# Sliding-window attention into a SwiGLU block: natural token order, 32-bit transposes, 128-row stores and a rebuilt start

## The chip, the cores and the metric

The kernel runs on one core of a Trainium2 chip. The metric is the device time of one execution in microseconds (us). Each run lists the execution that was profiled and several more; medians below are over all of them.

Names used below: TensorE (PE in the profile, with PEld for its weight loads), VectorE (DVE), ScalarE (ACT), GpSimd (POOL), SyncE (SP; its queue, which issues all the DMAs here, is SPq).

## The reference

```python
# q, k, v: (8, 8, 576, 64) fp32; window 64; weights (512, 1536) and (1536, 512)
scores = q @ k.transpose(0, 1, 3, 2) / sqrt(64)
rel = pos[:, None] - pos[None, :]
scores = where((rel >= 0) & (rel < 64), scores, -1e9)
attn = softmax(scores)
x = (attn @ v).transpose(0, 2, 1, 3).reshape(4608, 512)
g, val = x @ w_gate, x @ w_val
out = (g * sigmoid(g) * val) @ w_out
```

## The kernel before

The work is cut into 36 groups of 128 tokens (`NG`), 18 blocks of 256 tokens for loads of q, k, v (`NB`), and 9 tiles of 512 tokens for the feed-forward part. Everything is scheduled by hand: each engine runs its instructions in program order. After a start of about 147 us comes the main loop `for w in range(8, 36)`. One step of it does three gate/value column blocks, the projection of one earlier group, and the attention of a group four to six steps ahead.

To load two neighbouring tokens as one run of 512 bytes, partition r of a loaded block holds tokens 2r and 2r+1. This order (even tokens, odd tokens) goes through the whole kernel, up to the stores, which have to undo it:

```python
def load(n, src, nm, eng):
    ...
    eng.dma_start(
        x_f[o // 2:(o + m) // 2].rearrange("r h c d -> r h (c d)"),
        src[b, :, s:s + m, :].rearrange("h (r c) d -> r h (c d)", c=2),
    )

def turned(n, nm):                       # k and q of a block: 8 bf16 transposes each
    x_b = cast_qk.pop((nm, n))
    tp = ps_a.tile([P, 2, 4, P], BF16, name="tp", tag="a")
    for c in range(2):
        for p in range(4):
            nc.tensor.transpose(tp[:, c, p, :], x_b[:, c, P * p:P * p + P], identb[:])
    return tp

def products(g, via_pe=False):           # attention output of a group, then x turned
    ...
    if not via_pe:                       # groups 8 to 35
        sp.dma_start_transpose(out=xT[t][:, :, off:off + P], in_=x_b[:])
        return
    tp = ps_a.tile([P, 4, P], BF16, name="xtp", tag="a")   # groups 0 to 7
    for p in range(4):
        nc.tensor.transpose(tp[:, p, :], x_b[:, P * p:P * p + P], identb[:])
    act.copy(xT[t][:, :, off:off + P], tp[:])

def project(t, s, ps, tag):
    ...                                  # 12 matmuls of 512 columns, eviction by ScalarE
    n0 = 512 * t + P * s
    for i in range(2):
        sp.dma_start(
            out[n0 + 64 * i:n0 + 64 * i + 64, :].rearrange("(x c) f -> c x f", c=2),
            os_[64 * i:64 * i + 64, :],
        )
```

The softmax here doesn't subtract the row's maximum and nothing guards it: scores larger than these inputs give would overflow.

## Time and profile before

Median 452.41 us (three runs, 449.06 to 455.61). The profiled execution has a span of 452.1 us.

The main reading is by stretches: the start, the main loop with the last four projections, and the end after the last matmul. I date the boundary between start and loop by the first projection matmul inside the main loop, because it is easy to find.

| stretch | before |
|---|---|
| up to the first projection of the main loop | 153.4 us |
| from there to the last matmul | 279.8 us |
| after the last matmul | 19.0 us |

The first view is the table by stretches of the kernel before. Each line has the stretch, its length, then for each engine the busy time and number of instructions, then the granted TensorE clock (1.00 is full), the mean busy share of the 16 DMA engines, and GB/s.

```profile
core 0: us, PE busy (x) PEld busy (x) DVE busy (x) ACT busy (x) POOL busy (x), PEclk, DMA share, GB/s
0.00:147.00 147.00, 101.64 (x787) 70.00 (x788) 89.25 (x215) 48.38 (x97) 78.19 (x157) 0.86 0.67 163
147.00:433.00 286.00, 271.15 (x1736) 140.96 (x1733) 154.05 (x308) 103.04 (x172) 141.46 (x246) 0.97 0.46 93
395.00:433.00 38.00, 38.00 (x177) 17.11 (x175) 15.10 (x22) 10.15 (x17) 0.00 (x0) 1.00 0.11 36
433.00:452.00 19.00, 0.15 (x1) 0.00 (x0) 0.00 (x0) 0.60 (x1) 0.00 (x0) 0.57 0.12 48
```

Look at the last two lines. From 395 us on there is nothing left to load, and from 433 us on nothing left to compute. The stores alone are running, at a DMA share of 0.11 to 0.12. Two sixteenths are 0.125, so two of the sixteen engines work and fourteen idle. The Trainium skill says why ("DMA: Bandwidth & Descriptors", "Why a DMA increments its semaphore by 16 and not by 1"): a DMA is spread over the largest k up to 16 that divides the size of the slowest dimension on both sides. The store above has the slowest dimension `c`, of size 2. This trace agrees with that rule.

The next view is the instruction timeline of TensorE in the main loop of the kernel before. Columns: start, span of the piece (of a pipelined group, so use the differences of the starts), engine, line, what is computed, and the number of instructions.

```profile
205.48 0.61 PE L119 MATMUL tp<-identb,q_fb 128*128 128x128 bf16 x8
205.93 2.75 PE L273 MATMUL o_ps<-wo,hT 128*128 128x512 bf16 x12
208.51 1.03 PE L248 MATMUL g_ps<-xT,wg 128*128 128x512 bf16 x4
```

The eight bf16 transposes of a q block take 0.45 us from start to start (56 ns each), twelve matmuls of 512 columns 2.58 us. So TensorE is at its pace wherever nothing makes it wait. Where it does wait, the chain of waits shows a DMA transpose of x (columns: start, length, what):

```profile
223.69 0.70 DVE sg L259
...
224.61 7.57 DMA xT<-x_b
...
232.31 1.02 PE g_ps L248 x4
```

The queue of SyncE around the same time (start, length, what is issued) shows that the transpose is issued behind loads, and takes 4.46 us merely to be issued:

```profile
219.90 1.57 SPq L83 DMA_DIRECT2D q_f<-in_q_dram  x1
221.56 2.96 SPq L83 DMA_DIRECT2D v_f<-in_v_dram  x2
224.61 4.46 SPq L230 DMA_TRANSPOSE xT<-x_b  x1
229.16 1.09 SPq L281 DMA_DIRECT2D out_dram<-os__2762  x2
```

### The profile page before, as it was taken

The numbers are of one execution on the slowest core, as the hardware profiler recorded it, in microseconds if no ns is written. First come the engines' busy times: TensorE is split into PE (matmuls) and PEld (weight loads), VectorE is DVE, ScalarE is ACT, GpSimd is POOL, SyncE is SP. The second block draws the span as 40 slices with busy tenths as digits, with TensorE's granted clock in tenths as the row PEclk, the third lists the DMA queues.
The fourth block names the chain that finished last, engine by engine and source line by source line (L and its number), as shares of the span: only waits on it lengthen the run. The fifth ranks groups of instructions, "written<-read, shape, count | busy, mean of one in ns | idle before, by whom it ended". The sixth has DMA issues, their size and how long they took to land.

```text
span 452.1 us, 6976 instructions
## 1 busy us (share of the span) xinstructions
PE 372.9 (82%) x2520; PEld 211.0 (47%) x2520; DVE 243.3 (54%) x522; ACT 152.0 (34%) x270; POOL 219.7 (49%) x403
## 2 busy tenths in 40 slices
PE   2568689779853999699979988997999999999930
PEld 2355446556542555255535544553455554444410
DVE  5767868783431657266646554464457555646200
ACT  3243324424330343334424342433343433333210
POOL 6892330601997749464847554664648460000000
PEclk9988789889965999999999996999899999999975
DMA  8994809700599556615755763386363442211111
GB/s 254 323 261 161 259 0 259 162 1 20 158 71 184 142 129 129 134 47 133 138 116 117 103 131 87 109 102 130 81 130 85 52 51 38 45 36 33 38 48 45
DMA packets 82290, 51.30 MB, mean 113 GB/s; under 512 B 16720, under 2 KB 76112, under 8 KB 82256
## 3 DMA queue, kind: packets, MB, share of 16 engines
q1 hardware_dynamic: 82256, 50.87, 50.9%
q8 instruction: 19, 0.31, 0.3%
q14 instruction: 15, 0.12, 0.1%
HBM read 37.75 MB, written 9.44 MB: 104 GB/s over the span
## 4 chain that ended last, share of the span: by engine, by line
PE 54%; DMA 15%; DVE 10%; POOL 9%; ACT 3%; issue 3%; SPq 2%; POOLq 0%; DVEq 0%; ACTq 0%
PE g_ps L248 17%; PE v_ps L248 15%; PE o_ps L273 13%; DMA v_f<-in_v_dram 6%; DMA xT<-x_b 4%; PE ao_ps L219 4%; DMA k_f<-in_k_dram 3%; PE tp L119 2%; DMA out_dram<-os__4942 2%; DVE x_b L224 2%; POOL vbd_101 L108 2%; POOL E_102 L193 1%; SPq L83 1%; DVE sg L259 1%; POOL vbd_100 L108 1%
## 5 line engine op out<-in xcount | busy, mean ns | idle before, releaser
L259 DVE SCALAR_TENSOR_TENSOR sg<-th,g_ps 128x512 f32<-128x512 f32 (+1 forms) x123 | 76.5, 622 | 131.1 <-ACT th L253 130.5
L248 PE MATMUL g_ps<-xT,wg 128*128 128x512 bf16 (+1 forms) x492 | 120.9, 371 | 21.6 <-issue 7.5
L248 PE MATMUL v_ps<-xT,wv 128*128 128x512 bf16 (+1 forms) x492 | 118.7, 366 | 0.0
L253 ACT ACTIVATE th<-g_ps 128x512 f32<-128x512 f32 (+1 forms) x123 | 67.0, 545 | 142.0 <-PE g_ps L248 131.4
L273 PE MATMUL o_ps<-wo,hT 128*128 128x512 bf16 x432 | 98.6, 379 | 0.0
L264 DVE TENSOR_TENSOR hT<-sg,v_ps 128x512 bf16<-128x512 f32 (+1 forms) x123 | 76.3, 621 | 10.3
L248 PEld LDWEIGHTS <-wg 128*128 128x128 bf16 x492 | 48.8, 102 | 65.6 <-issue 18.5
L248 PEld LDWEIGHTS <-wv 128*128 128x128 bf16 x492 | 50.1, 102 | 50.1 <-issue 4.8
L273 PEld LDWEIGHTS <-hT 128*128 128x128 bf16 x432 | 41.2, 98 | 44.6
L224 DVE TENSOR_TENSOR x_b<-ao_ps,r 128x256 bf16<-128x256 f32 x72 | 30.6, 425 | 2.5
L108 POOL CAST vbd_98<-v_f 32x256 bf16<-32x256 f32 x48 | 20.5, 427 | 14.7 <-DMA v_f<-in_v_dram 12.9
L108 POOL CAST vbd_96<-v_f 32x256 bf16<-32x256 f32 x48 | 18.8, 393 | 17.8 <-DMA v_f<-in_v_dram 16.0
L193 POOL TENSOR_TENSOR E_102<-E_102,mask 128x512 bf16<-128x512 bf16 (+2 forms) x16 | 16.1, 1027 | 23.2 <-ACT E_102 L192 23.1
L108 POOL CAST vbd_100<-v_f 32x256 bf16<-32x256 f32 x48 | 18.9, 395 | 15.0 <-DMA v_f<-in_v_dram 13.2
L99 POOL CAST k_fb<-k_f 128x1024 bf16<-128x1024 f32 x16 | 16.6, 1037 | 19.1 <-DMA k_f<-in_k_dram 18.4
L223 DVE RECIPROCAL r<-ao_ps 128x4 f32<-128x4 f32 x72 | 12.7, 176 | 23.2 <-PE ao_ps L219 23.1
L193 POOL TENSOR_TENSOR E_104<-E_104,mask 128x512 bf16<-128x512 bf16 x14 | 15.8, 1149 | 16.5 <-ACT E_104 L192 16.4
L119 PE MATMUL tp<-identb,k_fb 128*128 128x128 bf16 x144 | 12.7, 240 | 12.8 <-DVE k_fb L99 7.8
L193 POOL TENSOR_TENSOR E_105<-E_105,mask 128x512 bf16<-128x512 bf16 x14 | 15.8, 1153 | 13.9 <-ACT E_105 L192 13.9
L193 POOL TENSOR_TENSOR E_103<-E_103,mask 128x512 bf16<-128x512 bf16 x14 | 15.8, 1153 | 12.5 <-ACT E_103 L192 12.5
L108 POOL CAST vbd_97<-v_f 32x256 bf16<-32x256 f32 x48 | 20.3, 423 | 2.2
L108 POOL CAST vbd_101<-v_f 32x256 bf16<-32x256 f32 x48 | 19.1, 399 | 2.2
(148 smaller groups left out, 450.1 us busy)
## 6 DMA issues: line engine op xcount, KB each, us to landing
k_f<-in_k_dram SPq DMA_DIRECT2D x12, 512.0 KB
q_f<-in_q_dram SPq DMA_DIRECT2D x12, 512.0 KB
v_f<-in_v_dram SPq DMA_DIRECT2D x12, 512.0 KB
w_f<-in_moe_w_gate_dram SPq DMA_DIRECT2D x4, 768.0 KB
w_f<-in_moe_w_val_dram SPq DMA_DIRECT2D x4, 768.0 KB
wo_f<-in_moe_w_out_dram SPq DMA_DIRECT2D x4, 768.0 KB
k_f<-in_k_dram SPq DMA_DIRECT2D x4, 384.0 KB
q_f<-in_q_dram SPq DMA_DIRECT2D x4, 384.0 KB
```

What stands on the lines that cost most here:

```text
L99: eng.tensor_copy(x, y)
L108: eng.tensor_copy(vb[64 * a + 32 * c:64 * a + 32 * c + 32, i % 2, :, 64 * a:64 * a + 64], v_f[32 * i:32 * i + 32, a::2, c, :],)
L119: nc.tensor.transpose(tp[:, c, p, :], x_b[:, c, P * p:P * p + P], identb[:])
L193: eng.tensor_mul(e, e, mask[:, lo:hi, :].unsqueeze(1).to_broadcast([P, 2, hi - lo, 64]))
L219: nc.tensor.matmul(o_ps[:, i, :], w, x, start=(n == 0), stop=(n == len(parts) - 1))
L223: dve.reciprocal(r[:], o_ps[:, :, P:VW])
L224: dve.tensor_mul(x_b[:, 256 * h:256 * h + 256].rearrange("r (p a d) -> r p a d", p=2, a=2), o_ps[:, :, 0:P].rearrange("r p (a d) -> r p a ...
L248: nc.tensor.matmul(ps[:, 0:n], w[:, c, P * m:P * m + P], xT[t][:, c, c0:c0 + n], start=(c == 0), stop=(c == 3),)
L253: act.activation(th[:, 0:n], g_ps[:, 0:n], AF.Tanh, scale=0.5)
L259: dve.scalar_tensor_tensor(sg[:, 0:n], th[:, 0:n], 1.0, g_ps[:, 0:n], ALU.add, ALU.mult)
L264: dve.tensor_mul(hT[t][:, m, c0:c0 + n], sg[:, 0:n], v_ps[:, 0:n])
L273: nc.tensor.matmul(o_ps[:], hT[t][:, c, P * s:P * s + P], wo[:, c, :], start=(c == 0), stop=(c == 11),)
```

## The change

The intent: keep tokens in natural order, so that a result tile is stored as 128 whole rows; pack two bf16 tokens into one 32-bit word, so that a block of q or k needs four fp32 transposes instead of eight bf16 ones; take the masks off GpSimd; turn all of x on TensorE; do the attention of four groups before the first gate/value work; and keep the TensorE clock up with dummy matmuls while the first loads run. Cut to its core:

```diff
-    KR, VR, ER, QR = 3, 6, 4, 3
+    KR, VR, ER, QR = 3, 3, 3, 3
-    wst = ctx.enter_context(tc.tile_pool(name="wst", bufs=4))
+    wst = ctx.enter_context(tc.tile_pool(name="wst", bufs=6))     # weights in 256-column pieces
+    def load_v(n):                                                # 256-byte runs
+        x_f = stage.tile([P, 2, H, D], FP32, name="v_f", tag="v_f")
+        for i in range(2):
+            for r, m, b, s, t in segments(256 * n + P * i, P, 1):
+                sp.dma_start(x_f[r:r + m, i], v[b, :, s:s + t, :].rearrange("h r d -> r h d"))
+    def pack(n, nm, eng):                                         # two tokens in one 32-bit word
+        x_w = cast.tile([P, H * D], FP32, name=nm + "w", tag=nm + "w")
+        y = x_w[:].bitcast(BF16).rearrange("r (h d c) -> r h c d", h=H, c=2)
+        ...copy x_f to y
     def turned(n, nm):
-        for c in range(2):
-            for p in range(4):
-                nc.tensor.transpose(tp[:, c, p, :], x_b[:, c, P * p:P * p + P], identb[:])
+        for p in range(4):
+            nc.tensor.transpose(tp[:, p, :], x_w[:, P * p:P * p + P], ident[:])   # fp32
@@ scores: mask multiplication on VectorE, with three masks for the sequence borders
-            eng.tensor_mul(e, e, mask[:, lo:hi, :]...)            # eng = pool from group 8 on
+            dve.tensor_mul(e, e, mk[:, 0:hi]...)
@@ products / turn_x
-        if not via_pe:
-            sp.dma_start_transpose(out=xT[t][:, :, off:off + P], in_=x_b[:])
-            return
+        xb[g] = x_b
+    def turn_x(g):                                                # all groups, placed later
+        ...4 bf16 transposes on TensorE, copy by ScalarE
@@ project
-        for i in range(2):
-            sp.dma_start(
-                out[n0 + 64 * i:n0 + 64 * i + 64, :].rearrange("(x c) f -> c x f", c=2),
-                os_[64 * i:64 * i + 64, :],
-            )
+        sp.dma_start(out[n0:n0 + P, :], os_[:])
@@ the start
+    warm(30)                                                      # 30 dummy matmuls
+    ...attention of groups 0 to 3, then gate/value of tile 0 with groups 4 to 6 woven in,
+    ...then tile 1 in two halves with projections of tile 0
@@ the main loop: scores 5 steps ahead (was 6), turn_x after the scores
```

## The prediction

> **What bounds the kernel now.** TensorE work, plus holes that DMA tears into it. The timeline by instruction shows the undisturbed pace: 12 matmuls of 512 columns in 2.59 us, products of one group 0.69, its scores 0.45, eight 128x128 transposes 0.45. Over the program (864 gate/value, 432 projection matmuls, 36 groups, 18 k/q blocks) this is some 340 us of the 452. An attended step of the main loop takes 9.34 us undisturbed, one without attention 7.77. The table by stretches:
> - 0 to 147 us (before the main loop): 70 to 75 us of such work; the clock is 0.79 to 0.86 after the first 25 us.
> - 147 to 433 us: 24 x 9.34 + 4 x 7.77 + 4 x 2.59 = 266 us of work, so 20 us of holes. In the chain of waits they are v, k, q loads and the DMA transposes of x (4 to 10 us each).
> - 433 to 452 us: TensorE is done; the last stores drain. The DMA share is 0.12, 2 of 16 engines. The Trainium skill, "DMA: Bandwidth & Descriptors", "Why a DMA increments its semaphore by 16 and not by 1": a DMA spreads over the largest k up to 16 that divides the slowest dimensions. These stores' slowest dimension is 2, and the trace agrees (36 to 48 GB/s). A 256 KB step so occupies two engines some 6 us of 9.3, ahead of loads that need all 16.
>
> **What the change does.**
> 1. Stores of 128 rows use 16 engines: the end falls from 19 to about 5 us (-14), and loads no longer queue behind two busy engines.
> 2. The 28 DMA transposes (SyncE 1.2 to 6.2 us to issue each) become TensorE transposes, 0.225 us per group (+6), and a ScalarE copy of 0.59 us (hidden). With 1, most of the holes go: -16.
> 3. Transposes of k, q: 288 bf16 become 144 fp32. I estimate 0.1 to 0.2 us each against 16 us before: 0 to +10. (The skill, "TensorE: Matmul & The Clock Gate", "Weight-path perf modes", excludes fp32 from the fast weight load; no trace here shows it yet.)
> 4. Masks to VectorE (0.47 to 0.56 us against 1.15 on GpSimd), 288 v casts become 72 larger ones: GpSimd from 220 to about 95 us. It was on the chain chiefly in the start.
> 5. The start is rebuilt: four groups of attention, then gate/value. I expect first gate/value at 25 to 28 us, the main loop at about 111 us instead of 147 (TensorE work alone gives 96; the rest waits for weights, k, q, v). The largest, least certain term: -36.
> 6. Against it: v moves in 256-byte pieces instead of 512[...]. A few us in the start, later nothing.
> 7. Dummy matmuls: under 2 us; the clock falls back before the first gate/value.
>
> **Sum.** 111 + 24 x 9.7 + 31 + 10.4 + 5 + 4 (left-over stalls) = 394 us. Range 380 to 414. Faster by over 2%: 0.97; within: 0.02; slower: 0.01.
>
> **What would show it.** Main loop begins near 111 us; TensorE over 97% busy and clock 1.0 from there; attended step 9.5 to 9.8 us; last matmul to end about 5 us; under 20 us of TensorE waits on DMA, in the start.
>
> **What would make it wrong.** fp32 transposes of 0.3 us or more (+15 to 30 us); 256-byte loads so slow that k, q, v fall behind; VectorE's order (normalising, masks, gate) stalling PSUM buffers each step; the start bound by DMA past 120 us.

## The result, and the profile after

The changed kernel runs in 389.28 us (median of 5, 388.02 to 391.72) against 452.41 us. The ratio is 0.8617, 95% interval 0.8561 to 0.8673. Ratios here are the mean time of one kernel's fast runs over that of the other's of the same rounds, so they are not quite the ratio of the medians that are quoted. The result is correct.

The profiled execution has a span of 390.0 us:

| stretch | before | after | difference |
|---|---|---|---|
| up to the first projection of the main loop | 153.4 us | 123.6 us | -29.8 |
| from there to the last matmul | 279.8 us | 262.2 us | -17.5 |
| after the last matmul | 19.0 us | 4.1 us | -14.8 |

(The differences are taken before rounding.)

The table by stretches of the changed kernel, with the same columns as before:

```profile
0.00:116.00 116.00, 96.92 (x758) 63.94 (x767) 82.39 (x188) 58.00 (x99) 39.82 (x56) 0.93 0.83 203
116.00:386.00 270.00, 267.85 (x1768) 145.22 (x1800) 179.71 (x333) 114.59 (x198) 54.72 (x64) 1.00 0.35 88
386.00:390.00 4.00, 0.00 (x0) 0.00 (x0) 0.00 (x0) 0.56 (x1) 0.00 (x0) 0.93 0.17 66
```

The end is 4 us long, the clock in the main loop is 1.00 (0.97 before), and TensorE is busy for 267.85 of 270 us. Asked for the waits of TensorE from 150 us to the end, the profile of the changed kernel gives none; that of the kernel before gives 14.9 us, all at the first gate/value matmul of a tile. This is its whole answer (who waited for whom, total us, times, longest):

```profile
PE g_ps L248 <- issue: 7.5, 2, 4.0
PE g_ps L248 <- DMA xT<-x_b: 7.4, 3, 3.3
```

The timeline of TensorE in the main loop of the changed kernel:

```profile
142.12 0.60 PE L111 MATMUL tp<-ident,q_fw 128*128 128x128 f32 x4
142.56 2.75 PE L252 MATMUL o_ps<-wo,hT 128*128 128x512 bf16 x12
145.15 1.03 PE L235 MATMUL g_ps<-xT,wg 128*128 128x512 bf16 x4
...
149.73 0.39 PE L199 MATMUL xtp<-identb,x_b 128*128 128x128 bf16 x4
149.96 1.03 PE L235 MATMUL g_ps<-xT,wg 128*128 128x512 bf16 x4
...
152.12 1.24 PE L252 MATMUL o_ps<-wo,hT 128*128 128x512 bf16 x5
```

Four fp32 transposes take 0.44 us (110 ns each), as long as the eight bf16 ones they replace (0.45 us). The four transposes of x take 0.23 us. A step takes 9.56 us (142.56 to 152.12); it took 9.34 before where nothing stalled.

The start is the part that I had explained least, so here is the chain of waits of its first 13 us in the changed kernel:

```profile
1.36 0.91 DVE kbd L277
...
2.44 0.93 DVE vbd L278
...
6.18 0.94 DVE vbd L300
...
7.72 0.94 DVE vbd L300
...
9.04 0.76 DVE k_fw L104
...
9.93 0.91 DVE kbd L307
...
11.01 0.91 DVE kbd L307
11.92 0.53 DVE kbd L120
```

VectorE clears tiles (lines 277, 278, 300, 307) before and after it packs the first k (line 104). In the kernel before, VectorE could start on the same k at 5.09 us, when it had landed; here it gets to it at 9.04 us. The chain names no wait for a load before 32 us. The first gate/value matmul comes at 28.9 us.

### The profile page after: what moved, and what is told of

Read it like the earlier page. It is cut to its first block, busy times and chain, and to the rows that moved or that the text cites. A ratio compares the mean times of both kernels' runs of the same rounds, so it can differ in the third digit from the quotient of the medians.

```text
span 390.0 us, 6619 instructions
## 1 busy us (share of the span) xinstructions
PE 364.8 (94%) x2524; PEld 209.2 (54%) x2566; DVE 262.1 (67%) x520; ACT 173.1 (44%) x296; POOL 94.5 (24%) x120
## 4 chain that ended last, share of the span: by engine, by line
PE 81%; DVE 8%; DMA 4%; ACT 3%; issue 2%; SPq 1%; POOL 1%; ACTq 0%; POOLq 0%; DVEq 0%
PE o_ps L252 24%; PE g_ps L235 21%; PE v_ps L235 21%; PE ao_ps L180 5%; PE tp L111 4%; DMA k_f<-in_k_dram 2%; PE xtp L199 2%; PE s_ps L157 2%; DVE E L162 2%; ACT E L161 2%; DMA v_f<-in_v_dram 1%; DVE x_b L185 1%; PE s_ps L156 1%; DVE kbd L120 1%; PE s_ps L159 1%
## 5 line engine op out<-in xcount | busy, mean ns | idle before, releaser
L252 PEld LDWEIGHTS <-hT 128*128 128x128 bf16 x432 | 42.2, 98 | 45.4
L162 DVE TENSOR_TENSOR E<-E,mask 128x512 bf16<-128x512 bf16 (+1 forms) x72 | 42.1, 589 | 24.0 <-ACT E L161 21.9
L104 POOL CAST k_fw<-k_f 128x1024 bf16<-128x1024 f32 x17 | 23.0, 1353 | 125.9 <-DMA k_f<-in_k_dram 87.0
L132 POOL CAST vbd<-v_f 64x512 bf16<-64x512 f32 x72 | 45.6, 634 | 24.1 <-DMA v_f<-in_v_dram 20.7
L161 ACT ACTIVATE E<-s_ps 128x512 bf16<-128x512 f32 (+1 forms) x72 | 38.7, 594 | 13.9 <-PE s_ps L159 13.0
L104 POOL CAST q_fw<-q_f 128x1024 bf16<-128x1024 f32 x17 | 23.2, 1362 | 60.2 <-DMA q_f<-in_q_dram 46.5
L180 PE MATMUL ao_ps<-vbd,E 128*128 128x130 bf16 x428 | 32.5, 226 | 3.7 <-DVE E L162 2.3
L180 PEld LDWEIGHTS <-E 128*128 128x128 bf16 x428 | 28.0, 100 | 12.9 <-DVE E L162 4.0
L120 DVE COPY kbd<-tp 64x1024 bf16<-64x1024 bf16 x36 | 24.6, 684 | 3.8 <-PE tp L111 3.5
L200 ACT COPY xT<-xtp 128x512 bf16<-128x512 bf16 x36 | 21.3, 591 | 8.5 <-PE xtp L199 8.4
L156 PE MATMUL s_ps<-qT,kbd 128*128 128x64 bf16 x144 | 20.1, 197 | 3.8 <-ACT qT L126 1.8
```

The lines of the kernel that those rows point to most:

```text
L104: eng.tensor_copy(y, x_f[:])
L120: dve.tensor_copy(kbd[n % KR][h, :, :, 64 * a:64 * a + 64], tp[h].rearrange("r p (b x) -> r p b x", x=64),)
L132: eng.tensor_copy(vbd[n % VR][64 * a:64 * a + 64, c:4:2, :, 64 * a:64 * a + 64], v_f[64 * c:64 * c + 64, :, a:8:2, :],)
L161: act.activation(e, s_ps[:, :, 0:hi, :], AF.Exp, scale=0.125)
L162: dve.tensor_mul(e, e, mk[:, 0:hi].unsqueeze(1).to_broadcast([P, 2, hi, 64]))
L180: nc.tensor.matmul(o_ps[:, i, :], w, x, start=(n == 0), stop=(n == len(parts) - 1))
```

## The experiments

Twelve kernels ran. The first four kernels with a and a_again, b_early and the two with c ran on the same chip. The first letter tells which kernel was edited: b for before, a for after (the changed one), c for the changed one with a further start. The table has the three stretches of each profiled execution; "start" ends with the first projection of the main loop.

| run | median us | ratio to before (95%) | start | loop | end |
|---|---|---|---|---|---|
| before (first profile) | 452.41 | 1 | 153.4 | 279.8 | 19.0 |
| b_store16 | 420.09 | 0.9271 (0.9213 to 0.9329) | 155.3 | 258.4 | 4.6 |
| b_petr | 448.71 | 0.9905 (0.9841 to 0.9969) | 156.1 | 271.9 | 19.2 |
| b_both | 434.09 | 0.9577 (0.9501 to 0.9654) | 156.3 | 271.9 | 4.8 |
| b_dvemask | 450.22 | 0.9945 (0.9874 to 1.0017) | 154.7 | 273.2 | 19.4 |
| b_early | 451.21 | 1.0023 (0.9968 to 1.0078) | 154.1 | 273.1 | 19.4 |
| after | 389.28 | 0.8617 (0.8561 to 0.8673) | 123.6 | 262.2 | 4.1 |
| a_again (the same) | 388.13 | 0.8621 (0.8576 to 0.8667) | 119.7 | 262.5 | 4.1 |
| a_store2 | 407.14 | 0.9054 (0.8995 to 0.9113) | 124.4 | 262.5 | 20.6 |
| a_dmatr | 383.49 | 0.8521 (0.8463 to 0.8580) | 119.1 | 259.0 | 4.0 |
| a_nowarm | 387.64 | 0.8614 (0.8552 to 0.8676) | 119.4 | 262.5 | 4.1 |
| a_v512 | 388.24 | 0.8637 (0.8576 to 0.8697) | 120.6 | 262.5 | 3.7 |
| c_start | 390.28 | 0.8672 (0.8618 to 0.8726) | 122.5 | 262.5 | 4.1 |
| c_best | 384.45 | 0.8543 (0.8501 to 0.8586) | 119.3 | 258.1 | 4.0 |

The start of the changed kernel varies by some 4 us between executions of the same program (123.6 and 119.7), so a single profile's start is not read more finely than that. Where nothing in the loop waits for DMA, kernels with the same loop agree within 0.3 us (262.2 to 262.5 us for the changed one, 271.9 us twice for b_petr and b_both). The loop of the kernel before varies more: b_dvemask and b_early leave its code as it is and took 273.2 and 273.1 us, against 279.8 us in the first profile. So what an edit of the kernel before gains in the loop is known to some 7 us only.

### b_store16: the stores of before on 16 engines

```diff
         for i in range(2):
-            sp.dma_start(
-                out[n0 + 64 * i:n0 + 64 * i + 64, :].rearrange("(x c) f -> c x f", c=2),
-                os_[64 * i:64 * i + 64, :],
-            )
+            rows = out[n0 + 64 * i:n0 + 64 * i + 64, :].rearrange("(x c) f -> c x f", c=2)
+            for c in range(2):
+                o = 64 * i + 32 * c
+                sp.dma_start(rows[c], os_[o:o + 32, :])
```

> The kernel before, with each 128-row result stored in four DMAs of 32 rows instead of two whose slowest dimension is 2: same rows, same order, but 16 engines each. Theory S (the two-engine stores make both the long end and most of the 20 us of holes in the main loop): end 19 to about 5 us, holes under 6 us, total about 422 to 428. Theory T (the DMA transposes of x make the holes, the stores only the end): end the same 5 us, holes stay at 14 us or more, total about 436 to 440. Neither touches the first 147 us.

Measured: 420.09 us, 32 us below the first median of before, from an edit that moves the same bytes in twice as many DMAs. Its end is 4.6 us, and its loop has no hole left (its longest wait is 0.2 us). The table by stretches (b_store16):

```profile
149.00:413.60 264.60, 262.91 (x1705) 139.18 (x1732) 153.52 (x308) 103.05 (x172) 141.69 (x246) 1.00 0.44 100
413.60:418.20 4.60, 0.02 (x1) 0.00 (x0) 0.00 (x0) 0.60 (x1) 0.00 (x0) 0.90 0.32 80
```

The same x transposes are still DMA transposes here, but SyncE now issues most of them in 1.2 us (the median of the 28; the longest took 3.95), between quicker loads (queue of SyncE, b_store16):

```profile
216.59 0.40 SPq L83 DMA_DIRECT2D q_f<-in_q_dram  x1
217.09 1.02 SPq L83 DMA_DIRECT2D v_f<-in_v_dram  x2
219.18 1.20 SPq L230 DMA_TRANSPOSE xT<-x_b  x1
224.11 1.74 SPq L284 DMA_DIRECT2D out_dram<-os__2784  x4
```

Compare 4.46 us for the issue of the transpose in the kernel before (median of its 28: 2.5 us, longest 6.2). So what theory S forecast came true, and the total lies even below its range of 422 to 428 us: with the same transposes and loads, stores on sixteen engines instead of two remove the holes. That the loads and transposes stood behind the stores engine by engine fits these issue times; the trace does not name the engines. This edit alone is about half of the whole gain (32 of 63 us).

A hole cost more than its own length. TensorE's waits in the loop of the kernel before add up to 14.9 us, but b_store16's loop is 21 us shorter. The rest shows as slower matmuls: TensorE is busy for 264.9 us in the loop of before and for 256.9 us in that of b_store16, with the same work, at a mean granted clock of 0.98 and 1.00. After the hole that ends at 316.89 us, for one, the granted clock was 0.60 for the next 3.7 us, and four gate matmuls took 1.89 us instead of 0.86. The loops of b_dvemask and b_early, with 12.7 and 12.4 us of waits, are 15 us longer than b_store16's.

### b_petr and b_both: x turned on TensorE, with the old and with the wide stores

```diff
-        if not via_pe:
-            sp.dma_start_transpose(out=xT[t][:, :, off:off + P], in_=x_b[:])
-            return
+        xb[g] = x_b
+        if via_pe:
+            turn_x(g)
+    def turn_x(g): ...                    # 4 transposes, as for groups 0 to 7
@@ main loop
             scores(w + 6, pool)
+        if w + 4 < NG:
+            turn_x(w + 4)
```

b_both has the stores of b_store16 as well.

> The kernel before, with all 36 transposes of x on TensorE (deferred behind the scores) and no DMA transpose; stores still on two engines. TensorE work rises by 28 x 0.225 = 6 us. Theory T: the holes of the main loop go (20 to under 4 us), total about 438, end still 17 to 20 us. Theory S: loads still wait behind stores on two engines, holes move to the loads and stay over 10 us, total 448 to 458.

> Both of the above. Both theories: main loop without holes, end about 5 us: 452 - 14 - 20 + 6 = 424 us. If they add up more than singly (S and T each cure the same holes), the sum of the single gains is larger than this one's.

Measured: 448.71 us and 434.09 us. The loops are 271.9 us in both: once x is turned on TensorE, nothing in the loop waits for DMA, even with the old stores. So each edit by itself cures the holes, and neither theory was complete: the holes need the two-engine stores and the DMA transposes together. Theory S's forecast for b_petr (holes move to the loads) was wrong; that the total lies in its range (448 to 458 us) has another reason, the end of 19.2 us that stays and the new waits told of below. How much the missing holes are worth in b_petr is not clear: its loop is 8 us shorter than in the first profile of before, but only 1 us shorter than in b_dvemask and b_early. The forecast for b_both, 424 us, was missed by 10 us.

But turning x on TensorE is not free. With the stores cured, it lengthens the loop from 258.4 to 271.9 us and the kernel from 420.09 to 434.09 us. The waits of TensorE from 150 us on in b_both show part of it:

```profile
PE tp L119 <- ACT E L192: 5.9, 20, 0.3
```

The k or q transposes that follow wait 20 times 0.3 us for a PSUM buffer of the pool `ps_a` (three buffers, now with one more user in each step). Some 5.4 us are the transposes themselves (24 steps of 0.225 us), so 5.4 + 5.9 of the 13.5 us are accounted for; about 2 us are not.

### b_dvemask and b_early: why is the end of the old start slow?

b_dvemask:

```diff
-    scores(8, pool, 1, 4)          # and scores(9) to scores(13)
+    scores(8, dve, 1, 4)
```

> The kernel before, with the 12 masks of the groups 8 to 13 (ahead of the main loop) on VectorE instead of GpSimd, nothing else. Theory P (GpSimd, 32 of 47 us busy between 100 and 147 us, holds up the end of the start): the main loop begins 8 to 13 us earlier, total about 440 to 444. Theory D (that part of the start waits for k, q and v from memory): the main loop begins less than 3 us earlier, total over 449.

Measured: 450.22 us, ratio 0.9945 with an interval that includes 1; the start ends at 154.7 us. GpSimd was named by the chain of waits, but taking work from it moved the wait to the next thing. TensorE's waits between 105 and 155 us, first in the kernel before, then in b_dvemask:

```profile
PE ao_ps L219 <- POOL E_102 L193: 5.1, 2, 4.8
PE tp L119 <- POOL k_fb L99: 5.0, 3, 4.0
```

```profile
PE tp L119 <- POOL k_fb L99: 8.7, 1, 8.7
```

The wait for the cast of k (`k_fb`) is now a wait for a load: GpSimd, idle for 5.86 us, casts the k of block 7 at 143.44 us, when it has landed. SyncE issues this load only at 135.1 us, behind the loads of block 6 (116 us, after the stores of the first two projections), the stores of two more and two DMA transposes, of which the second took 4.05 us to issue. b_early keeps the masks on VectorE and issues the loads of blocks 6 and 7 and k and q of block 8 one block earlier:

```diff
         casts_v(4, i, pool)
+    loads(6)
...
         casts_v(5, i, pool)
-    loads(6)
+    loads(7)
```

> The kernel before, with the masks of groups 8 to 13 on VectorE, and the loads of blocks 6, 7 and of k, q of block 8 issued one block earlier, ahead of the stores of the projections instead of behind them. Theory L (the end of the start waits for loads that SyncE issues only after the first two projections are stored, at 113 us, with memory idle between 92 and 105 us; moving the masks alone therefore bought nothing): the main loop begins 8 us or more earlier (its first projection under 146 us instead of 153 to 155), total under 444. Rival (neither GpSimd nor the loads set the pace; the order of the work on TensorE does): less than 4 us earlier, total over 446.

Measured: 451.21 us, ratio 1.0023; the start ends at 154.1 us. The loads of block 6 were indeed issued at 84 us, those of block 7 from 117 us on. The wait for the k of block 7 shrank to 2.8 us, and a third wait, of 6.5 us, appeared, for the DMA transpose of the last group before the main loop (TensorE's waits from 105 to 155 us, b_early):

```profile
PE g_ps L248 <- DMA xT<-x_b: 6.5, 1, 6.5
PE tp L119 <- POOL k_fb L99: 2.8, 1, 2.8
```

Both theories L and P failed in the form in which I stated them. The numbers of their rivals came true (theory D: over 449 us; the rival of L: over 446), but the traces name neither the loads alone nor the order of TensorE's work. There are at least three limits within a few us of each other, and two of them were taken away for nothing. What the rebuilt start gains, about 30 us, was not taken apart further: neither the masks, nor the masks with earlier loads, nor wide stores, nor x on TensorE shortens the old start by itself. Which combination does is open, and so is the most obvious rival: the new order of the work (four groups of attention first) was not tried by itself. What the two tables by stretches show is that most of it is idle time: TensorE is idle for 45.4 of the first 147 us before and for 19.1 of the first 116 us after; its granted clock there is 0.86 and 0.93.

### a_store2: the old stores in the changed kernel

The store statement of before was put back; rows come out permuted, so the result is wrong.

> The changed kernel with the stores of before (two DMAs with slowest dimension 2; the output rows come out permuted, wrong on purpose). End of span: 4 to about 19 us under every theory, total at least 403. Theory S for the main loop: loads wait behind the stores, holes of 5 us or more come back, total over 408. Theory T: without DMA transposes the main loop has slack, holes under 3 us, total 402 to 407.

Measured: 407.14 us. The end grows from 4.1 to 20.6 us, and the loop stays at 262.5 us. This is the forecast of theory T, and it fits what b_petr showed: without DMA transposes, TensorE does not notice the two-engine stores until the end. In the changed kernel the wide stores are worth about 18 us (407.14 less 389.28); in the kernel before, the corresponding edit was worth 32.

### a_dmatr: DMA transposes of x in the changed kernel

```diff
         x_b = xb.pop(g)
+        if g >= 8:
+            sp.dma_start_transpose(out=xT[t][:, :, off:off + P], in_=x_b[:])
+            return
```

> The changed kernel with the x of groups 8 to 35 turned by DMA as before (28 DMA transposes), stores on 16 engines. TensorE loses 6 us of work. Theory T: holes at the first gate/value matmul of each 512 tokens come back, 10 us or more, total 393 to 405. Theory S: with stores out of the way the transposes land in time, total 383 to 389, so that the TensorE transposes were a loss.

Measured: 383.49 us, correct. The loop is 259.0 us, 3.3 us less, and TensorE's only wait in it of any size is for VectorE (waits of TensorE from 116 to 378 us, a_dmatr):

```profile
PE g_ps L238 <- DVE hT L250: 1.2, 1, 1.2
```

So turning x on TensorE, one of the aims of the change, was a small loss once the stores were wide. Against the control a_again, which ran later on the same chip, the total is 4.6 us less, and the single runs do not overlap (381.8 to 385.3 against 387.2 to 388.4 us). What is not in the loop lies in the start, within its scatter. The pair c_start and c_best below repeats the comparison.

### a_nowarm and a_v512: dummy matmuls, and 256-byte pieces

a_nowarm leaves out `warm(30)`. a_v512 loads v like k and q, in runs of 512 bytes, and casts from it as if the tokens were in natural order (wrong result).

> The changed kernel without the 30 dummy matmuls. They end at 10.8 us and the first k is packed at 9.8 us, so they delay the first transpose by about 1 us. Theory W (they keep the clock up for the first attention): slower by 1 to 3 us without. Theory N (the clock has fallen again before it matters; VectorE's clearing of tiles sets the pace): within 1 us, or up to 1.5 us faster without.

> The changed kernel with v loaded in 512-byte pieces of two tokens, as k and q are, and cast from the same tile as if it were in natural order (wrong result on purpose). Theory V (256-byte pieces cost DMA time in the start, where its share is over 1 between 29 and 70 us): v loads take about half as long there, the wait of GpSimd for k of block 3 at 42 to 48 us shrinks by 3 us or more, total 384 to 387. Rival: DMA time is hidden, total within 1 us of 389.

Measured: 387.64 us (0.8614) and 388.24 us (0.8637), against 0.8617 and 0.8621 for the unchanged kernel. Neither differs from it by more than the scatter. Theory N holds for the dummies: without them TensorE just waits for the first k (waits of TensorE up to 29 us, a_nowarm):

```profile
PE tp L111 <- DVE k_fw L104: 9.9, 1, 9.9
```

and the first gate/value matmul comes at 28.4 instead of 28.9 us. Theory V falls: the smaller pieces cost no time that can be seen in the total. They do cost DMA time, and it is hidden: the packets took 49.5% of the 16 engines' 386.3 us in a_again and 45.9% of 386.7 us in a_v512, which is 191 and 178 us per engine.

### a_again, c_start and c_best: a control, and an attempt to do better

> The changed kernel once more, unchanged, as the control for the other three on the same chip: 388 to 391 us. Its first 124 us vary: the profiled run began its second projection stage some 4 us later than the runs without dummy matmuls or with wide v loads.

> The changed kernel with a shorter start: no dummy matmuls; k of block 0 is cast and turned before VectorE clears the tiles of blocks 1 and 2; the transposes of block 3 and the attention of groups 6 and 7 come one to three steps later, behind the time at which their loads land. Theory C (the first 29 us wait for VectorE's clearing): first gate/value at 23 to 25 us instead of 28.9; and the 2.8 us wait for k of block 3 goes. If DMA is full from 0 to 70 us anyway and sets the pace, the gain at the end is smaller: total 383 to 387. Rival (the start is bound by DMA alone): total 388 to 391.

> The same, with x of groups 8 to 35 turned by DMA as before, which bought 4 to 6 us in the changed kernel. If the two gains add: 378 to 383 us, faster than both kernels; main loop from the first projection to the last matmul 259 us.

c_start moves VectorE's clearing and drops the dummies:

```diff
-    for i in range(VR): ...clear vbd[i]...
-    warm(30)
     pack(0, "k_f", dve)
     pack(0, "q_f", act)
-    for kb in kbd[1:]:
-        dve.memset(kb[:], 0.0)
-    cast_v(0, pool)
     turn_k(0)
     turn_q(0)
+    ...masks, cast_v(0)
     scores(0)
     scores(1)
+    dve.memset(kbd[1][:], 0.0); dve.memset(vbd[1][:], 0.0)   # block 2 still later
@@ block 3: turn_k at m=9 (was 7), turn_q at 10 (was 9); scores(6) at 11; groups 6, 7 later
```

c_best adds the DMA transposes of a_dmatr.

Measured: the control 388.13 us, c_start 390.28 us, c_best 384.45 us. c_start is 2 us slower than the control (single runs 389.0 to 392.8 against 387.2 to 388.4 us), so theory C failed as I built it. The first k is turned at 5.8 us instead of 9.9, but the first gate/value matmul comes at 30.1 us, later than the 28.9 of the control. TensorE's waits up to 29 us in c_start:

```profile
PE tp L111 <- DVE k_fw L104: 5.8, 1, 5.8
PE ao_ps L180 <- DVE x_b L185: 3.9, 2, 3.5
```

The second line is one reason: the clearing of block 1 now stands on VectorE between the masks and the normalisation of group 0 (`x_b`), and takes some 2.4 us there. The four mask multiplications before it are another: they took 3.71 us, against 2.26 in the control; why is not shown. The clearing was moved within the chain, not out of it. The 2.8 us wait for the k of block 3 did go, but TensorE's waits for VectorE's gate (`sg`) in the first 124 us grew from 3.9 us in the control to 8.4. The total fits the rival of theory C (a start bound by DMA alone, 388 to 391 us), but that is not shown either: a_v512, with less DMA time, did not shorten the start (120.6 us). c_best missed its forecast of 378 to 383 us, since c_start brought nothing to add.

c_best against c_start is a clean pair for the transposes of x: 0.8543 (0.8501 to 0.8586) against 0.8672 (0.8618 to 0.8726). The intervals do not meet; DMA transposes are 5.8 us faster, 4.3 of them in the loop. a_dmatr and c_best both beat the kernel before and the changed kernel; the simplest of them, a_dmatr, has the lowest median, 383.49 us.

## Why the prediction was right or wrong, point by point

The forecast was 394 us with a range of 380 to 414; measured 389.28. The direction and the size were right. The terms were less exact than the sum: errors of about 5 to 9 us cancelled, which was luck.

1. **Stores (-14 at the end): right.** The end went from 19.0 to 4.1 us (-14.8). The statement that loads queue behind the stores fits the issue times (two v loads took 2.96 us to issue, 1.02 in b_store16), but loads alone open no holes (b_petr); the DMA transposes issued on the same queue do. This part was at least as large: b_store16 took 15 to 21 us from the loop of the kernel before as well (by which of its executions one compares).
2. **DMA transposes to TensorE ("with 1, most of the holes go"): right in the sum, wrong in the cause.** The holes go, but wide stores alone remove them (b_store16: loop 258.4 us, no waits). After that the TensorE transposes only cost: 3.3 us of loop in the changed kernel (a_dmatr), 4.3 in the pair c_start and c_best. The forecast of +6 us for their work was about right for the loop (5.4 us of work); what I failed to see is that this price bought nothing.
3. **fp32 transposes (0 to +10): 0.** 110 ns each, four in 0.44 us against eight bf16 in 0.45 us. The Trainium skill ("TensorE: Matmul & The Clock Gate", "Weight-path perf modes — Fast Weight Load (FWL) and DoubleRow") leaves fp32 out of the fast weight load, and the records agree (mean weight load 145 ns against 105 to 108 for the bf16 ones of k and q before), but half as many instructions make up for it.
4. **GpSimd (220 to about 95 us): right, and worth little.** It fell to 94.5 us. That it was on the chain in the start was true of the profile and did not mean that relieving it helps: b_dvemask gained nothing that can be told from zero.
5. **The start (-36): the direction right, the size 5 us too large.** First gate/value at 28.9 us (forecast 25 to 28), main loop at 116.5 us (forecast 111), first projection of the loop 29.8 us earlier than before. The reason I gave for its length, waiting for weights and k, q, v, is wrong for the first 29 us: there the chain runs through VectorE's clearing and the attention of four groups in series. It holds further on: the transpose of k of block 3 waits 2.8 us for a load at 49 us, in a stretch with a DMA share above 1.
6. **256-byte pieces of v ("a few us in the start"): not seen.** a_v512 lies within the scatter of the control; the 13 us of DMA time per engine that the pieces cost over the program are hidden.
7. **Dummy matmuls (under 2 us): right;** a_nowarm lies within the scatter. The clock fell back as forecast: in the changed kernel it was 1.00 from 1.5 to 11 us, 0.82 from 11 to 21 and 0.59 from 21 to 29 us, just before the first gate/value.

The main loop balanced the start: I had put an attended step at 9.7 us and 4 us of left-over stalls; measured are 9.56 us and none. From the start of the main loop to the last matmul I had 24 x 9.7 + 31 + 10.4 + 4 = 278 us; it took 269.4 us (116.5 to 385.9), 8.6 less. The start took 5.5 us more, the end 0.9 less: 394 + 5.5 - 8.6 - 0.9 = 390.0, the profiled span.

## What to carry to other kernels

Look at the DMA share in a stretch where only one kind of transfer runs: 0.12 there meant two engines of sixteen, and rewriting the store so that the slowest dimension of each DMA is 32 instead of 2 was worth 32 us of 452. When two changes cure the same wait, try each alone: here the cheap one sufficed, and the other then only cost TensorE time. A wait named by the profile may hide a second and a third of equal length, so relieving one engine can change the name of the wait and not the time.

## What the Trainium skill lacked or had wrong

- "DMA: Bandwidth & Descriptors" gives the rule for the number of engines, but not what a small k does to others: with stores on 2 engines (36 to 48 GB/s) a DMA transpose took up to 6.2 us to issue (median 2.5) and one stood in the chain for 7.6 us; with stores on 16 engines the median was 1.2 us and the longest 3.95, and the kernel gained 32 us.
- The same page asks for at least 512 bytes for full rate (Specifications). The DMA time agrees (191 us per engine with v in 256-byte runs, 178 with 512-byte runs), but in this kernel that time is hidden: the total shows no difference (0.8617 and 0.8621 against 0.8637).
- "TensorE: Matmul & The Clock Gate" ("Part 4: PE-mode transpose") gives 275 to 390 ns for a 128x128 bf16 transpose. Back to back in this kernel they start every 56 ns at a granted clock of 1.00; only the recorded span of a single one is 230 to 280 ns. The page has no duration for fp32: 110 ns each here.
